# Second product of the next to last tile by seven block products, with the sums kept on the chip

## The chip, the cores and the metric

One NeuronCore of a Trainium2 chip runs the whole kernel. Time is device time in microseconds (us) of that core, as a median of several executions. TensorE (PE in the profile) multiplies matrices into PSUM; VectorE (DVE), ScalarE (ACT) and GpSimd (POOL) do what is elementwise; SyncE (SP) starts the transfers. Each engine works through its own queue in order and waits on semaphores for the others.

## The reference

Attention over 8 batches of 8 heads, 576 positions and 64 dimensions, with a causal window of 128 and a slope of the head on the distance, and behind it a feed-forward layer on all 4608 tokens:

```python
scores = scale * np.matmul(q, k.transpose(0, 1, 3, 2))
mask = (rel >= 0) & (rel < window)
scores = np.where(mask, scores + bias[None], -1000000000.0)
attn = np.exp(scores - np.max(scores, axis=-1, keepdims=True))
attn = attn / (np.sum(attn, axis=-1, keepdims=True) + 1e-09)
x = np.matmul(attn, v)                      # as 4608 tokens x 512
h = x @ w_in                                # 512 -> 2048
g = 0.5 * h * (1.0 + erf(h * inv_sqrt2))
out = (g @ w_out).astype(np.float32)        # 2048 -> 512
```

## The kernel before

The tokens are cut into nine tiles of 512 (`TT`), numbered `t` = 0 to 8. While tile t goes through the feed-forward layer, attention of the next batch is worked in between its steps, so that TensorE always has something to do; tiles 7 and 8 have no attention beside them any more. Every float32 operand of a product is split into a high and a low float16 half, and a product is made of three: high by high, low by high, high by low. The low half is `value * scale - high`, one instruction on VectorE (`low_part`, line 149 in the profile).

A tile's first product (`mlp_in`, line 600) makes 16 blocks `h` of 128 features by 512 tokens, 12 matmuls of 512 columns each, in four PSUM buffers that take turns (tag `mm`). ScalarE turns `h` into `g32` by Gelu and, in tile 7, into the high half too (lines 623, 627); VectorE makes the low half. The second product (`mlp_out`, line 661) makes 4 blocks of 128 tokens by 512 outputs, 48 matmuls of 512 columns each: 192 in a tile.

Tile 8 (`t == FAST`, `seven_all`) is different. Both of its products treat the operands as 2 by 2 blocks and take seven products of (sums of) blocks in place of eight. For that it needs, beside the blocks themselves:

- sums of the blocks of `w_in`, called T1 to T4, in four parts `d` = 0 to 3 (`sums_of_weights`);
- sums of the blocks of `w_out`, likewise (`sums_of_weights_out`), laid into buffers that attention no longer needs (`qbuf`, `kbuf`, `vbuf`, `e_main`);
- sums of the tile's own `x` (`sums_of_x`) and of its features (`Seven.sum`: S1 to S4).

A sum is built by adding high and low half to float32, four subtractions, a cast to the high half on ScalarE and a subtraction for the low half on VectorE. In the kernel before, all adds and subtractions are VectorE's. `sums_of_weights` writes its halves to a buffer in device memory (`stored`); from there T1 is copied over the block of `w_in` that it replaces, and T2, T3 and T4 are read back part by part (`stream`) while tile 8 runs. These calls are spread over tile 6's end and tile 7 by a list of steps (`PARTS_AT`, `SUMS_AT`). Inside `seven_all`, `p1` to `p7` are the seven products of a part of the first product (12 matmuls of 256 columns each); `u` and `v` are their PSUM buffers, and `p6` adds to `u` what `p1` has left there, so it has to wait until ScalarE has copied `u` out (line 826). The second product follows as seven products of 48 matmuls of 256 columns (line 901).

A scheduler that works from the code's order and its own estimates sets the order of each engine's queue; waits come from which tile is read and written.

Of the kernel before, what the change touches and what calls it, by code (L numbers as in the profile page):

```python
# [57 lines left out]
def attention_gelu_mlp(  # L58
# [520 lines left out]
    def tile_scales(t, ns):  # L579
# [7 lines left out]
        nc.vector.tensor_scalar(sg, sww[:, r], sx[t], 2.0 ** -(22 if t >= FAST else 21), op0=ALU.mult, op1=ALU.mult)  # L587
# [5 lines left out]
    def mlp_in(t, fc):  # L593
# [50 lines left out]
    o_ps = {}

    def mlp_out(t, tb, fc, first=0, last=NFC - 1):
# [18 lines left out]
        if fc == last:  # L665
# [4 lines left out]
            else:  # L670
# [9 lines left out]
    sums, streams, rooms, slots = [], [], [], []  # L680
    sums_out = [e.rearrange(p)[:, 0 : 8 * 512].rearrange("p (a k s f) -> p a k s f", a=2, k=2, s=4)
                for e, p in ((qbuf, "p a s -> p (a s)"), (kbuf, "p a s -> p (a s)"),
                             (vbuf, "p a h n d -> p (a h n d)"), (e_main, "p g a k -> p (g a k)"))]
# [21 lines left out]
    def sums_of_blocks(name, blocks, order, gate=None):  # L705

        r = pool.tile([P, NG, W], F32, tag="s", name=f"t{name}", bufs=2)
        r = r.rearrange("p g k -> p (g k)")[:, 0:1024].rearrange("p (s f) -> p s f", s=4)
# [11 lines left out]
        return r  # L720

    def halves_of_sums(dst, r):
        nc.scalar.copy(dst[0], r)
        nc.vector.tensor_tensor(out=dst[1], in0=r, in1=dst[0], op=ALU.subtract)
# [433 lines left out]
```

## Time and profile before

| | |
|---|---|
| median of 3 executions | 944.19 us (943.04 to 946.74) |
| the profiled execution | 947.36 us, of which the span from first to last instruction is 945.3 us |
| granted TensorE clock, mean | 0.984 of full speed |
| PE busy | 909.2 us, 96% of the span |
| DVE busy | 720.3 us, 76% |
| ACT busy | 546.5 us, 58% |
| POOL busy | 194.2 us, 21% |

A group `L661 PE MATMUL o<-wo,g 128*128 128x512 f16 x12` is line 661's matmuls that write tile `o` from `wo` and `g`, 128 partitions by 512 columns each, twelve in a row. In the timeline the first number is when the first of them began (us from the span's start), the second how long until the last ended; in brackets stands how long the engine had waited and for whom. Matmul ends are modelled, so the time from one start to the next is what is read of PE. [...]

### The profile page before, as it was taken

What the parts mean: (1) busy time and instruction counts of PE and PEld (TensorE: products, weight loads), DVE (VectorE), ACT (ScalarE), POOL (GpSimd) and SP (SyncE); (2) the same over time, 40 slices, a digit from 0 to 9 for tenths busy, and PEclk for the clock granted to TensorE, in tenths of its full rate; (3) what the DMA queues carried; (4) which work ended last, traced back from release to release, by engine and by line L of the source; (5) the groups of instructions that cost most, each with busy time, mean ns of one, the idle gap of its engine ahead of it and who ended that gap; (6) DMA issues with size and microseconds to landing.
All of it is one profiled execution on the core that took longest, in us unless ns stands there. A gap on an engine that the chain in (4) does not pass through costs nothing.

```text
span 945.3 us, 18563 instructions
## 1 busy us (share of the span) xinstructions
PE 909.2 (96%) x7356; PEld 475.2 (50%) x7356; DVE 720.3 (76%) x1445; ACT 546.5 (58%) x1146; POOL 194.2 (21%) x412
## 2 busy tenths in 40 slices
PE   6969999789999899999999999999999999999998
PEld 3544444444454345444454445444544444445887
DVE  6798989779876877678767877787656799991771
ACT  5977967776673565356435643564465526731760
POOL 1010000013101443135313531163125420000000
PEclk9889999999999999999999999999999999999999
DMA  9518532972446124614562346225302554300201
GB/s 317 212 45 259 209 105 67 203 191 61 90 126 165 36 57 83 187 43 79 96 162 68 62 101 174 69 51 99 86 13 51 91 116 146 90 34 23 79 24 45
DMA packets 185527, 99.63 MB, mean 105 GB/s; under 512 B 133344, under 2 KB 165216, under 8 KB 185312
## 3 DMA queue, kind: packets, MB, share of 16 engines
q1 hardware_dynamic: 185440, 98.45, 41.3%
q8 instruction: 57, 0.93, 0.4%
q14 instruction: 30, 0.25, 0.1%
HBM read 50.72 MB, written 13.63 MB: 68 GB/s over the span
## 4 chain that ended last, share of the span: by engine, by line
PE 68%; DVE 7%; ACT 5%; DMA 4%; issue 2%; SPq 1%; DVEq 0%; ACTq 0%
PE o L661 31%; PE h L600 22%; PE av L559 4%; PE sc L415 4%; DMA v<-vp 2%; PE u L789 2%; PE u_out L901 2%; PE v L789 2%; DMA et<-e_main 1%; ACT s L510 1%; DVE stv L217 1%; DVE vbuf L149 1%; DVE nmax L507 1%; ACT L623 1%; ACT vbuf L337 1%
## 5 line engine op out<-in xcount | busy, mean ns | idle before, releaser
L600 PE MATMUL h<-x,wi 128*128 128x512 f16 x1536 | 344.7, 382 | 6.5 <-ACT g L623 3.0
L661 PE MATMUL o<-wo,g 128*128 128x512 f16 x1080 | 244.7, 379 | 1.1 <-DVE wo L149 1.1
L600 PEld LDWEIGHTS <-wi 128*128 128x128 f16 x1536 | 148.2, 98 | 188.0 <-issue 14.2
L661 PEld LDWEIGHTS <-g 128*128 128x128 f16 x1440 | 136.0, 98 | 164.6 <-issue 3.0
L510 ACT ACTIVATE s<-s,nmax 128x192 f32<-128x192 f32 x252 | 111.2, 443 | 103.1 <-DVE nmax L507 99.5
L623 ACT ACTIVATE g<-h,gs 128x512 f32<-128x512 f32 x112 | 74.8, 685 | 81.0 <-PE h L600 57.4
L149 DVE SCALAR_TENSOR_TENSOR g<-g,sg,g 128x512 f16<-128x512 f32 (+1 forms) x128 | 101.9, 811 | 22.6 <-POOL g L625 19.4
L625 POOL TENSOR_SCALAR g<-g,sg 128x512 f16<-128x512 f32 x96 | 78.5, 823 | 193.4 <-ACT g L623 189.6
L149 DVE SCALAR_TENSOR_TENSOR e_main<-s,z,e_main 128x192 f16<-128x192 f32 x252 | 107.4, 469 | 14.1 <-POOL e_main L519 9.6
L519 POOL TENSOR_SCALAR e_main<-s,z 128x192 f16<-128x192 f32 x180 | 87.6, 506 | 85.4 <-ACT s L510 29.0
L415 PE MATMUL sc<-kbuf,qbuf 64*64 64x192 f16 (+1 forms) x1656 | 74.3, 261 | 9.8 <-DMA kbuf<-kp 4.5
L661 PE MATMUL o<-wo_first,g 128*128 128x512 f16 x360 | 83.2, 380 | 0.3 <-DMA wo_first<-wo 0.3
L437 DVE SCALAR_TENSOR_TENSOR s<-sc,cs,bias_h 128x384 f32<-128x384 f32 x112 | 63.7, 607 | 12.8 <-PE sc L415 12.6
L507 DVE TENSOR_REDUCE nmax<-s 128x5 f32<-128x960 f32 (+1 forms) x56 | 58.5, 1044 | 2.2 <-POOL s L442 0.2
L442 POOL MEMSET s<- 64x128 f32 (+1 forms) x112 | 19.2, 172 | 186.4 <-DVE s L437 185.7
L572 ACT ACTIVATE x<-av,cx 128x448 f16<-128x448 f32 (+6 forms) x52 | 23.6, 474 | 58.4 <-PE av L559 58.2
L415 PEld LDWEIGHTS <-qbuf 64*64 64x64 f16 x1512 | 35.9, 106 | 38.2 <-issue 35.5
L559 PE MATMUL av<-et,vbuf 128*64 128x128 f16 (+1 forms) x1680 | 45.2, 213 | 4.2 <-DMA et<-e_main 4.2
L559 PEld LDWEIGHTS <-vbuf 128*64 128x64 f16 x1680 | 42.1, 113 | 14.3 <-issue 9.0
L510 ACT ACTIVATION_READ_ACCUMULATOR s<-s,nmax 128x1 f32 x252 | 47.2, 187 | 0.0
L510 ACT ACT_TABLE_LOAD x29 | 37.2, 1283 | 7.8 <-DVE square L120 7.3
L623 ACT ACT_TABLE_LOAD x29 | 37.2, 1283 | 6.4 <-issue 2.9
(224 smaller groups left out, 1029.0 us busy)
## 6 DMA issues: line engine op xcount, KB each, us to landing
v<-vp SPq DMA_DIRECT2D x32, 320.0 KB, 5.1
out<-ob SPq DMA_DIRECT2D x35, 256.0 KB, 2.2
raw<-w_in SPq DMA_DIRECT2D x8, 1024.0 KB, 14.0
raw<-w_out SPq DMA_DIRECT2D x8, 1024.0 KB, 5.7
q<-qp SPq DMA_DIRECT2D x7, 1152.0 KB, 6.1
k<-kp SPq DMA_DIRECT2D x7, 1152.0 KB, 6.6
stored<-ts SPq DMA_DIRECT2D x32, 128.0 KB, 2.2
room<-stored SPq DMA_DIRECT2D x12, 256.0 KB, 2.7
```

The source lines that it names most:

```text
L149: nc.vector.scalar_tensor_tensor(out=dst, in0=src, scalar=scale, in1=high, op0=ALU.mult, op1=ALU.subtract)
L415: nc.tensor.matmul(ps[bank][o, n, 0:W], a, m, start=(i == 0), stop=(i == len(terms) - 1 and b > 0), skip_group_check=True,)
L437: nc.vector.scalar_tensor_tensor(out=s[:, bank[0] : bank[0] + k, :], in0=ps[bank][:, 0:k, 0:W], scalar=cs, in1=bias.broadcast_to([P, k, W] ...
L507: nc.vector.tensor_reduce(out=nmax[:, r], in_=s[:, r], axis=AX.X, op=ALU.max, negate=True)
L510: nc.scalar.activation(s[:, i, :], s[:, i, :], AF.Exp, bias=nmax[:, i : i + 1], accum_out=z[:, i : i + 1])
L519: nc.gpsimd.tensor_scalar(e[:, i, 0, c], s[:, i], z[:, i : i + 1], 1.0, op0=ALU.mult, op1=ALU.mult)
L559: nc.tensor.matmul(av[r, (j - blocks[0]) * QB : (j - blocks[0] + len(js)) * QB], v32s[b][:, hp, kb, r] if b < EXACT else vbuf[:, vi, hp, k ...
L600: nc.tensor.matmul(ph, wi[n][:, a, cc, k * P : (k + 1) * P], x[:, cc, b, :], start=(i == 0), stop=(i == 3 * NCC - 1),)
L623: nc.scalar.activation(g32, ph, AF.Gelu, scale=gsc[t, n])
L625: nc.gpsimd.tensor_scalar(g[:, r, 0], g32, gsg[t, n], 1.0, op0=ALU.mult, op1=ALU.mult)
L661: nc.tensor.matmul(o, both[:, a, c], wo[n][:, b, k, :], start=(fc == first and i == 0), stop=(fc == last and i == 2),)
L789: nc.tensor.matmul(ps[:, k * HT : (k + 1) * HT], w(a, i)[:, k * P : (k + 1) * P], m(b, i),  start=first and n == 0, stop=True, skip_group_ ...
```

## The change

The second product of tile 7 is also taken by seven products of blocks (`FAST_OUT = 7`, `seven_out`, which `seven_all` now shares): 336 matmuls of 256 columns where 192 of 512 stood. Tile 7's features go through a new `features`, which keeps them in float32 until a part is complete, then makes three of its four halves and four sums, S1 to S4. The sums of `w_out` are needed a tile earlier and are now all taken at the end of tile 6 and the start of tile 7. The sums of `w_in` may only be made once tile 7's first product has read `w_in`, so `sums_of_weights` runs during `seven_out(7)`, and `stored` and the transfers to and from it are gone: T1 goes straight into its place, T2 to T4 into free stretches of ten buffers (`room_for_halves`, `piece`). In `sums_of_blocks` one of the two adds goes to GpSimd, and all of `sums_of_x` but its last instruction does.

```diff
@@ tile_scales, features, out_scale
+FAST_OUT = 7
-        nc.vector.tensor_scalar(sg, sww[:, r], sx[t], 2.0 ** -(22 if t >= FAST else 21), op0=ALU.mult, op1=ALU.mult)
+        nc.vector.tensor_scalar(sg, sww[:, r], sx[t], 2.0 ** -(22 if t >= FAST else 23 if t >= FAST_OUT else 21), op0=ALU.mult, op1=ALU.mult)
+        if t >= FAST_OUT:
+            Sums(t, q).features(r, ph)
+            return
         g32 = pool.tile([P, TT], F32, tag="ob", name=f"g32_{t}_{fc}", bufs=3)
         nc.scalar.activation(g32, ph, AF.Gelu, scale=gsc[t, n])
-        if t + 1 < FAST:
-            nc.gpsimd.tensor_scalar(g[:, r, 0], g32, gsg[t, n], 1.0, op0=ALU.mult, op1=ALU.mult)
-        else:
-            nc.scalar.activation(g[:, r, 0], g32, AF.Copy, scale=gsg[t, n])
+        nc.gpsimd.tensor_scalar(g[:, r, 0], g32, gsg[t, n], 1.0, op0=ALU.mult, op1=ALU.mult)
...
-    stored = dram.tile([4, NWP // 2, P, 2, 2, 256], F16, name="stored")
...
+    def sums_of_blocks(first, second, quarter, dst, gate=None):
+        r = [turns[m].rearrange("p (j f) -> p j f", j=first[0].shape[1]) for m in range(2)]
         if gate is not None:
-            nc.vector.tensor_copy(r[:, 0, 0:1], gate)
-        for m, b in enumerate(blocks):
-            nc.vector.tensor_tensor(
-                out=r[:, 2 * m : 2 * m + 2], in0=b[0], in1=b[1], op=ALU.add
-            )
-        b11, b12, b21, b22 = (r[:, n] for n in order)
+            for m in range(2):
+                nc.vector.tensor_copy(r[m][:, 0, 0:1], gate)
+        for m, b in enumerate((first, second)):
+            engine = nc.gpsimd if m else nc.vector
+            engine.tensor_tensor(out=r[m], in0=b[0], in1=b[1], op=ALU.add)
+        b11, b12, b21, b22 = (quarter(r, n) for n in range(4))
         nc.vector.tensor_tensor(out=b11, in0=b12, in1=b11, op=ALU.subtract)
         nc.vector.tensor_tensor(out=b12, in0=b22, in1=b12, op=ALU.subtract)
         nc.vector.tensor_tensor(out=b22, in0=b22, in1=b11, op=ALU.subtract)
         nc.vector.tensor_tensor(out=b21, in0=b21, in1=b22, op=ALU.subtract)
...
+        for n, v in ((T1, b11), (T3, b12), (T2, b22), (T4, b21)):
+            hi, lo = dst(n)
+            nc.scalar.copy(hi, v)
+            nc.vector.tensor_tensor(out=lo, in0=v, in1=hi, op=ALU.subtract)
...
     def sums_of_x(t, i):
         x = x_tile(t)[:, 2 * i : 2 * i + 2]
-        r = pool.tile([P, 2, TT], F32, tag="v32", name=f"r{t}_{i}", bufs=1)
-        nc.vector.tensor_tensor(out=r, in0=x[:, :, 0], in1=x[:, :, 1], op=ALU.add)
+        r = next_of(pairs).rearrange("p (c n) -> p c n", c=2)
+        nc.gpsimd.tensor_tensor(out=r, in0=x[:, :, 0], in1=x[:, :, 1], op=ALU.add)
...
+        nc.gpsimd.tensor_tensor(out=a22, in0=a21, in1=a22, op=ALU.add)
+        nc.gpsimd.tensor_tensor(out=a21, in0=a11, in1=a21, op=ALU.subtract)
+        nc.gpsimd.tensor_tensor(out=a11, in0=a22, in1=a11, op=ALU.subtract)
+        nc.gpsimd.tensor_tensor(out=a12, in0=a12, in1=a11, op=ALU.subtract)
...
+        def features(self, r, ph):
+            t, d = self.t, self.d
+            hi, k = divmod(r, 2)
+            if k == 0:
+                held32[d, hi] = next_of(pairs).rearrange("p (k f) -> p k f", k=2)
+            v = held32[d, hi]
+            nc.scalar.activation(v[:, k], ph, AF.Gelu, scale=gsc[t, 2 * d])
+            if k == 0:
+                return
+            if hi == 0:
+                self.halved(0, 0, v[:, :, 0:HT])
+                return
+            a11, a21 = (held32[d, 0][:, :, n * HT : (n + 1) * HT] for n in range(2))
+            a12, a22 = (v[:, :, n * HT : (n + 1) * HT] for n in range(2))
+            self.halved(1, 0, a12)
+            self.halved(1, 1, a22)
+            self.three(a11, a21, a22)
+            self.sum(S4, a12, a12, a11, ALU.subtract)
...
+        if t >= FAST_OUT:
+            rest_of_v = room_for_features()
+            for fc in range(NFC):
+                mlp_in(t, fc)
+                if fc in PARTS_AT:
+                    sums_of_weights_out(parts.pop(0))
+                if fc in SUMS_AT:
+                    sums_of_x(t + 1, SUMS_AT.index(fc))
+            room_for_halves(rest_of_ld, rest_of_v)
+            for n, _ in enumerate(seven_out(t)):
+                if n + 1 < NWP // 2:
+                    sums_of_weights(n)
+                if n == 6:
+                    turns[:] = later[2:4]
+                    sums_of_weights(NWP // 2 - 1)
+            continue
```

Up to the last softmax of attention no engine's queue changes. Three places behind it matter. The first is VectorE's queue where tile 8 starts. Its first instruction there is the sum of tile 8's first block (before: line 831, after: line 886, `room_s<-v,room_s`). Before, this stood ahead of it, the last sums of `w_out` and the last output block of tile 7:

```order
L717 TENSOR_TENSOR to_1_10210<-to_1_10210 128x256
L718 TENSOR_TENSOR to_1_10210<-to_1_10210 128x256
L719 TENSOR_TENSOR to_1_10210<-to_1_10210 128x256
L724 TENSOR_TENSOR e_main<-to_1_10210,e_main 128x1024
L671 TENSOR_SCALAR ob_2_10207<-o_2_10149,so_9650 128x512
L831 TENSOR_TENSOR room_s_10293<-v_0_10316,room_s_10293 128x512
```

After, the sums of `w_in` of part 3 and three of tile 7's output blocks stand there (750 to 753 are the four subtractions, 757 the low halves, 973 the output):

```order
L750 TENSOR_TENSOR slots_9623<-slots_9623 128x2x256
L973 SCALAR_TENSOR_TENSOR ob_1_0_10310<-x_out,so_9619,room_s_9621 128x512
L973 SCALAR_TENSOR_TENSOR ob_1_1_10313<-y_out,so_9619,room_s_9621 128x512
L751 TENSOR_TENSOR slots_9623<-slots_9623 128x2x256
L757 TENSOR_TENSOR wi_770<-slots_9623,wi_770 128x2x256
L752 TENSOR_TENSOR slots_9623<-slots_9623 128x2x256
L757 TENSOR_TENSOR vbuf<-slots_9623,vbuf 128x512
L753 TENSOR_TENSOR slots_9623<-slots_9623 128x2x256
L757 TENSOR_TENSOR bias_h<-slots_9623,bias_h 128x512
L973 SCALAR_TENSOR_TENSOR ob_0_1_10379<-z_out,so_9619,room_s_9622 128x256 x2
L757 TENSOR_TENSOR e_main<-slots_9623,qbuf 128x512
L886 TENSOR_TENSOR room_s_9621<-v_0_10408,room_s_9621 128x512
```

The sums of `w_in` have moved from the first half of tile 7 to right ahead of tile 8, on the queue that tile 8's first sum has to pass.

The second place is ScalarE's queue at the same point of the program. Before, the copy of `u` that `p6` waits for (line 826) came behind the last output block of tile 7:

```order
L723 CAST e_main<-to_0_10174 128x1024
L669 ACTIVATE ob_1_10137<-o_1_10079,so_9650 128x512
L723 CAST e_main<-to_1_10210 128x1024
L669 ACTIVATE ob_3_10284<-o_3_10219,so_9650 128x512
L826 COPY room_s_10293<-u_0_10302 128x512
```

After, the same copy (now line 881) comes behind the casts of the sums of `w_in` (line 756):

```order
L756 CAST slots_9625<-room_s_9621 128x512
L969 ACTIVATE room_s_9621<-u_out,so_9619 128x512
L756 CAST wi_770<-slots_9623 128x2x256
L756 CAST vbuf<-slots_9623 128x512
L756 CAST bias_h<-slots_9623 128x512
L756 CAST qbuf<-slots_9623 128x512
L881 COPY room_s_9621<-u_0_10394 128x512
L871 ACTIVATE room_s_9621<-room_s_9621,gs_0_10384 128x512
```

The cast of `qbuf` needs VectorE's line 753 of part 3, so the copy of `u` now stands behind the whole of VectorE's queue up to there.

The third place is the end of GpSimd's queue. Before, its last work was attention's (line 519):

```order
L442 MEMSET s_3_9216 64x128 x2
L442 MEMSET s_3_9216 64x64 x2
L519 TENSOR_SCALAR e_main<-s_3_9216,z_3_9313 128x192 x9
L1154 UNCONDITIONAL_BRANCH
L1154 ISA
```

After, 18 instructions with two tensor operands follow it: four adds for `w_out`, two sums of `x` of five instructions each, four adds for `w_in`. This is the middle of them (748 is the add of `sums_of_blocks`, 779 to 784 are `sums_of_x`):

```order
L748 TENSOR_TENSOR room_9583<-wo_1563 128x1024
L748 TENSOR_TENSOR room_9583<-wo_1683 128x1024
L779 TENSOR_TENSOR room_s_9621<-x_8841 128x1024
L781 TENSOR_TENSOR room_s_9621<-room_s_9621 128x256
L782 TENSOR_TENSOR room_s_9621<-room_s_9621 128x256
L783 TENSOR_TENSOR room_s_9621<-room_s_9621 128x256
L784 TENSOR_TENSOR room_s_9621<-room_s_9621 128x256
L779 TENSOR_TENSOR room_9584<-x_8841 128x1024
```

GpSimd had nothing to do from there to the end of the program before.

## Rows read from the trace of the kernel before

**Rows 1.** The page, span and busy time of each engine.

```profile
span 945.3 us, 18563 instructions
PE 909.2 (96%) x7356; PEld 475.2 (50%) x7356; DVE 720.3 (76%) x1445; ACT 546.5 (58%) x1146; POOL 194.2 (21%) x412
```

**Rows 2.** Busy time by stretch: tile 7's two products, tile 8 in halves, end.

```profile
core 0: us, PE busy (x) PEld busy (x) DVE busy (x) ACT busy (x) POOL busy (x), PEclk, DMA share, GB/s
785.20:826.60 41.40, 41.40 (x194) 18.75 (x193) 41.11 (x73) 29.99 (x40) 0.00 (x0) 1.00 0.43 128
826.60:868.00 41.40, 41.40 (x193) 18.81 (x192) 24.70 (x43) 9.02 (x10) 0.00 (x0) 1.00 0.07 26
868.00:905.70 37.70, 37.70 (x347) 33.75 (x345) 25.16 (x39) 27.40 (x45) 0.00 (x0) 1.00 0.25 71
905.70:941.50 35.80, 35.80 (x329) 31.91 (x326) 14.75 (x22) 10.39 (x16) 0.00 (x0) 1.00 0.07 23
941.50:945.30 3.80, 0.06 (x1) 0.00 (x0) 0.88 (x2) 0.00 (x0) 0.00 (x0) 1.00 0.20 69
```

**Rows 3.** Timeline of PE from tile 7 on (start, length, group).

```profile
826.60 2.75 PE L661 MATMUL o<-wo_first,g 128*128 128x512 f16 x12
...
868.04 1.47 PE L789 MATMUL u<-x,wi 128*128 128x256 f16 x12
...
872.18 1.47 PE L789 MATMUL u<-room,room 128*128 128x256 f16 x12
...
922.73 0.82 PE L901 MATMUL u_out<-qbuf,slots 128*128 128x256 f16 x6
...
927.97 0.82 PE L901 MATMUL y_out<-vbuf,slots 128*128 128x256 f16 x6
```

**Rows 4.** Timeline of ACT, first copy of tile 8.

```profile
869.60 0.59 ACT L826 COPY room_s<-u 128x512 f32<-128x512 f32 x1 [0.68 <-PE u L789]
```

**Rows 5.** Timeline of DVE from attention's end to tile 8's features.

```profile
766.67 0.18 DVE L514 RECIPROCAL z<-z 128x4 f32<-128x4 f32 x1
...
793.81 2.35 DVE L724 TENSOR_TENSOR ts<-ti,ts 128x1024 f16<-128x1024 f32 x2
796.08 0.42 DVE L760 TENSOR_TENSOR r<-r 128x256 f32<-128x256 f32 x1
...
839.21 0.68 DVE L712 TENSOR_TENSOR to<-wo 128x512 f32<-128x512 f16 x1
839.81 0.74 DVE L671 TENSOR_SCALAR ob<-o,so 128x512 f32<-128x512 f32 x1
840.47 1.88 DVE L712 TENSOR_TENSOR to<-wo 128x512 f32<-128x512 f16 x3
...
912.59 0.69 DVE L819 TENSOR_TENSOR room_s<-room_s 128x512 f32<-128x512 f32 x1
913.31 0.69 DVE L819 TENSOR_TENSOR room_s<-s,room_s 128x512 f32<-128x512 f32 x1
...
915.18 1.40 DVE L149 SCALAR_TENSOR_TENSOR slots<-room_s,sg,slots 128x512 f16<-128x512 f32 x2
916.51 0.74 DVE L149 SCALAR_TENSOR_TENSOR g<-room_s,sg,g 128x512 f16<-128x512 f32 x1
```

**Rows 6.** Timeline of DVE in tile 5, low halves with POOL at work.

```profile
623.30 4.47 DVE L149 SCALAR_TENSOR_TENSOR g<-g,sg,g 128x512 f16<-128x512 f32 x4
```

**Rows 7.** Timeline of POOL, the same stretch, and one instruction ahead of it.

```profile
614.14 0.69 POOL L625 TENSOR_SCALAR g<-g,sg 128x512 f16<-128x512 f32 x1 [2.37 <-ACT g L623]
...
622.38 2.65 POOL L625 TENSOR_SCALAR g<-g,sg 128x512 f16<-128x512 f32 x3
625.35 0.79 POOL L625 TENSOR_SCALAR g<-g,sg 128x512 f16<-128x512 f32 x1 [0.31 <-ACT g L623]
626.45 0.78 POOL L625 TENSOR_SCALAR g<-g,sg 128x512 f16<-128x512 f32 x1 [0.31 <-ACT g L623]
```

More of the change, by code (lines that the diff above doesn't have):

```diff
@@ L672, in mlp_out @@
             nc.sync.dma_start(out[t * TT + tb * P : t * TT + (tb + 1) * P, :], ob)
-    stored = dram.tile([4, NWP // 2, P, 2, 2, 256], F16, name="stored")
     S2, S3, S4, S1 = range(4)
     T2, T3, T4, T1 = range(4)
[L680 to L683, printed above, removed]
+    sums, rooms, slots, turns, later, pairs, pieces = ([] for _ in range(7))
@@ L685, in room_for_sums @@
     def room_for_sums():
-        a, b = (pool.tile([P, NPAIR * S], F32, tag="ld", name=f"room{n}", bufs=2).bitcast(F16) for n in range(2))
+        a, b = (flat("ld", [P, NPAIR, S], F32, f"room{n}", 2) for n in range(2))
+        turns.extend(a[:, n * 1024 : (n + 1) * 1024] for n in range(2))
+        pairs.extend(b[:, n * 1024 : (n + 1) * 1024] for n in range(2))
+        a, b = a.bitcast(F16), b.bitcast(F16)
         x = a[:, 0 : 4 * NCC * HT].rearrange("p (i a s f) -> p i a s f", i=2, a=2, s=4)
@@ L700, in room_for_features @@
-        where.append(pool.tile([P, NPAIR, NKB, P], F32, tag="v32", name="slots2", bufs=1)
-                     .rearrange("p h n d -> p (h n d)").bitcast(F16))
+            pairs.append(s[:, 0:1024])
+            later.append(s[:, 0:1024])
+        where = [flat(f"et{n}", [P, NG * 4, P], F16, f"slots{n}", 1) for n in range(2)]
+        where.append(flat("v32", [P, NPAIR, NKB, P], F32, "slots2", 1).bitcast(F16))
+        later.extend(where[0].bitcast(F32)[:, n * 1024 : (n + 1) * 1024] for n in range(2))
@@ new lines, in room_for_halves @@
+    def room_for_halves(b, v):
+        x = pool.tile([P, NCC, 2, TT], F16, tag="x", name="room_x", bufs=2).rearrange("p c a f -> p (c a f)")
+        h = bias_h.rearrange("p h k -> p (h k)").bitcast(F16)
+        n = 512
+        halves = [(e[:, at : at + n], e[:, at + n : at + 2 * n]) for e, ats in (
+            (b, range(0, 8 * n, 2 * n)), (x, range(0, 8 * n, 2 * n)), (v, [8 * n]), (h, [0]), (spare[2], [8 * n]),
+        ) for at in ats]
+        halves.append((spare[0][:, 8 * n : 9 * n], spare[3][:, 8 * n : 9 * n]))
+        pieces.extend([a.rearrange("p (i f) -> p i f", i=2) for a in piece] for piece in halves)
+        turns[:] = later[0:2]
@@ L719, in sums_of_blocks @@
         nc.vector.tensor_tensor(out=b21, in0=b21, in1=b22, op=ALU.subtract)
[L720 to L724, printed above, removed]
-    def sums_of_weights(d, i, gate=None):
-        r = sums_of_blocks(f"i{d}_{i}", [
-            [wi[2 * d + m][:, a, 2 * i : 2 * i + 2] for a in range(2)] for m in range(2)
-        ], (0, 2, 1, 3), gate)
-        st = pool.tile([P, NG * 4, P], F16, tag=f"et{i}", name=f"ts{d}_{i}", bufs=1)
-        st = st.rearrange("p n f -> p (n f)")[:, 0:2048].rearrange("p (a s f) -> p a s f", a=2, s=4)
-        halves_of_sums([st[:, a] for a in range(2)], r)
-        for n, k in ((T1, 0), (T2, 3), (T3, 2), (T4, 1)):
-            nc.sync.dma_start(stored[n, d, :, :, i], st[:, :, k])
@@ L885, in seven_all, with seven_out @@
             q[d].p7()
-            if d < last:
-                stream(T3, d + 1)
+        for _ in seven_out(t, q[last]):
+            pass
+    def seven_out(t, rest=None):
+        last, every = NWP // 2 - 1, range(NWP // 2)
         ps = {}
@@ L1063, in attention_gelu_mlp @@
     SCORES_AT, WEIGH_AT = (2, 11, 16, 21), (12, 20, 25, 30)
-    PARTS_AT, SUMS_AT = (1, 3, 6, 9, 12, 15, 17, 19, 21, 23, 25, 27), (28, 29)
-    parts = [lambda d=d, i=i, gate=None: sums_of_weights(d, i, gate) for d in range(NWP // 2) for i in range(2)]
-    parts += [lambda d=d, k=k: sums_of_weights_out(d, k) for d in range(NWP // 2) for k in range(2)]
+    PARTS_AT, SUMS_AT = (2, 6), (10, 14)
+    parts = list(range(NWP // 2))
     for t in range(1, NTILE):
```

178 lines of the change are left out of this document (93 added, 85 removed).

## The prediction

> **What bounds the kernel now.** I read first the busy time of each engine [rows 1]: TensorE is busy for 909.2 of 945.3 us, VectorE for 720.3. That is a mean over stages, so I cut the part that the change touches into stretches [rows 2]. [...] VectorE is nearly full too in tile 7's first product, 41.11 of 41.40 us, and has room only in its second, 24.70 of 41.40. GpSimd does nothing at all from 785.20 on. So the gain is TensorE's in the second product of tile 7, and what can eat it is VectorE, to which the change gives more to do and less time to do it in.
>
> **What is removed.** The timeline of TensorE [rows 3] has tile 7's second product from 826.60 to 868.04, 41.44 us for 192 matmuls of 512 columns. Its seven products are 336 matmuls of 256 columns. Tile 8's second product has the same ones already: one product of 48 runs from 922.73 to 927.97, 5.24 us. Seven take 36.68 us, so TensorE's own time falls by 4.76 us. The transfers to and from the stored sums go as well; nothing on TensorE waits for one [rows 2], so I count them at nothing.
>
> **What VectorE has to do, and by when.** All sums and tile 7's features now stand in VectorE's queue between attention's last softmax and the start of tile 8. The end of this stretch is a chain: ScalarE's first copy of tile 8 (line 881, which `p6` waits for) stands behind the cast of part 3's last sum, and that cast waits for VectorE's line 753 of part 3.
>
> The time there is. It begins where VectorE has the last softmax's reciprocal, 766.67 and 0.18 long [rows 5]: 766.85, the gate of the first new sum. In the trace `p6` starts at 872.18, 4.14 us after tile 8's first matmul at 868.04 [rows 3]. Tile 8 would now start 4.76 us earlier, at 863.28, and want `p6` at 867.42. Ahead of that lie the copy, 0.59 us [rows 4], and a cast of as many elements, which I price the same. So line 753 has to end by 866.24, and VectorE has 99.4 us.
>
> The work. Prices are from one start to the next [rows 5]: 1.14 us for 1024 columns (two from 793.81 to 796.08), 0.60 for 512 with two tensors in (839.21 to 839.81), 0.66 for a low half (915.18 to 916.51 has two) or an output block (839.81 to 840.47). By the code, the queue up to there holds:
> - 10 of 1024 columns: eight adds of blocks and the two last instructions of `sums_of_x`: 11.4 us;
> - 78 of 512: 32 subtractions of weight sums, 30 of their low halves (two of part 3 come later), 16 sums of features: 46.8 us;
> - 28 low halves of tile 7's features, seven in each part: 18.5 us;
> - 16 left-overs: eight of attention, five output blocks, three of a few columns: about 6.9 us.
>
> Together 83.6 us. A subtraction that directly follows the one whose result it needs starts 0.72 us behind it (912.59 to 913.31), not 0.60. If all 48 subtractions did, this would be 5.8 us more; I reckon with a dozen and take 85.0 us, with 83.6 and 89.4 as ends. That fits into 99.4 with 14.4 to spare.
>
> **GpSimd beside it.** The change also wakes GpSimd in this stretch, and the trace shows that the two do not work beside each other for free. Alone, a low half follows another after 0.66 us, so four would take 2.72 us to the end of the last (three steps and its 0.74). With GpSimd at work four took 4.47 us [rows 6], 1.75 more; GpSimd ran four multiplications of 512 columns beside them, two of the three at 622.38 and those at 625.35 and 626.45, and these were slower too, 0.88 us for one of the three where one alone takes 0.69 [rows 7]. So each of GpSimd's instructions cost VectorE 0.44 us, or 0.86 ns per column, and they take turns. That instruction reads one tensor; the new ones read two, and the trace has none such. GpSimd gets eight adds of 1024 columns, and twice `sums_of_x` with one of 1024 and four of 256: 12,288 columns. If only the columns count, VectorE loses 10.6 us; if every tensor read does, 21.1 us. I take the second: if the two engines take turns at reading, the row prices one tensor read, and an add has two. Both ends stay for the range; a cost below the first would need an add that is cheaper than a multiplication, and nothing is gained from GpSimd beyond the instructions that I have left out of VectorE's list.
>
> One thing more: four adds for `w_in` have VectorE's first subtraction waiting for their result. GpSimd needs 0.69 us alone for what costs VectorE 0.44, so I add 0.25 for each, 1.0 us.
>
> By this VectorE needs 85.0 + 21.1 + 1.0 = 107.1 us of 99.4, and is late by 7.7 us. TensorE then waits for as long, mostly at `p6` of tile 8. A part of the lateness can show earlier, and is then not paid twice, since whatever TensorE waits in tile 7 moves the later date as well.
>
> [...]
>
> **Sum.** 7.7 - 4.76 = +2.9 us. The profiled execution took 947.36 us, the median of the three shown is 944.19; the change is the same length in both, so 950.3 for the one and 947.1 for the other. With VectorE's work at its ends it is 1.5 to 7.3 us more than before: 945.7 to 951.5.
>
> **Rivals.**
> - *VectorE is in time.* If an add costs VectorE only by its columns, it needs 85.0 + 10.6 + 1.0 = 96.6 us of 99.4, TensorE never waits, and all 4.76 us are gained: 939.4. For it: VectorE's list alone leaves 14.4 us, and parts of the sums could fall into gaps. Against it: the row of four low halves. The point where it turns is a cost to VectorE of 13.4 us for all of GpSimd's work, 1.1 us for an add of 1024.
> - *GpSimd holds VectorE for longer.* In the rows a multiplication costs VectorE 0.44 us and lasts 0.69 alone. If with two tensors the loop inside takes longer and the cost lies midway, at 0.565 us per 512 and tensor, 12,288 columns cost 27.1 us, VectorE is 13.7 late, and the kernel takes 8.9 us more: 953.1. With the full 0.69 it would be 33.1 us and 959, which I hold for unlikely, since the two overlapped in the row. [...]
> - *It bites before tile 8.* VectorE's queue runs through the low half of `x7`'s last pair, which the first block's last matmul needs, and through the sums of part 2, whose casts stand ahead of tile 7's first Gelu on ScalarE. Should VectorE be late there, TensorE waits in tile 7's first product. By itself that adds nothing, as said; only a wait of another kind, say a Gelu that finds no free buffer among the four of `pairs`, would come on top, 1 to 3 us: about 949.
>
> **How the numbers follow.** 0.5% is 4.7 us and about what a measurement of this kernel can tell from no change. My own case has 0.50; about 0.15 of it lies over 948.9, the rest within 0.5%. The longer hold has 0.20, all slower. VectorE in time has 0.25: at 939.4 it sits just at the lower bound, 939.5, so I give 0.10 to faster and 0.15 to within. The extra wait in tile 7 has 0.05, slower. That makes faster 0.10, within 0.50, slower 0.40. The range reaches from the full gain, 939.4, past the longer hold with some of VectorE's upper end, 955. The likeliest case alone is 945.7 to 951.5.
>
> **What the profile after would show.** Right: line 948's 336 matmuls take 36.7 us plus waits; TensorE, without a gap before, has one of some 8 us at tile 8's first `p6` (line 861) or spread over tile 7, and the chain of waits there leads over ScalarE to VectorE; GpSimd's adds of 1024 last about 2 us; low halves and subtractions beside them last clearly over 0.75 us. Wrong: adds of about 1.3 us and VectorE's instructions at their usual length, with no gap on TensorE; then the first rival holds. If VectorE is hardly slowed and still late, my list of its work was short; if GpSimd's add lasts over 2.5 us, the second rival holds.

## The result, and the profile after

The changed kernel takes 948.75 us (median of 16 executions, 946.6 to 953.03), the kernel before 944.54 us beside it (16 executions). The ratio is 1.0044, with a 95% interval of 1.003 to 1.0057: 4.2 us more. The forecast was 2.9 us more. The profiled execution took 946.64 us, 944.9 of them span. In it tile 7 begins at 779.29, not at 785.16; TensorE's work ahead of that is the same in both kernels and differed between two executions. So I compare by stage: from the start of tile 7 to the end it is 165.6 us here (944.9 - 779.29) and 160.1 before (945.3 - 785.16), 5.5 us more in this one execution (by the interval of the ratio it is 2.8 to 5.4). Tile 7's first product, before and after:

```profile
785.16 41.60 PE L600 MATMUL h<-x,wi 128*128 128x512 f16 x192
779.29 41.60 PE L600 MATMUL h<-x,wi 128*128 128x512 f16 x192
```

The page, against [rows 1]: VectorE has 22.0 us more, GpSimd 32.9, TensorE 6.2 less.

```profile
span 944.9 us, 18800 instructions
PE 903.0 (96%) x7500; PEld 488.1 (52%) x7500; DVE 742.3 (79%) x1427; ACT 556.4 (59%) x1175; POOL 227.1 (24%) x430
```

Busy time by stretch, against [rows 2]: tile 7's two products, then tile 8, and last a piece of the second product.

```profile
core 0: us, PE busy (x) PEld busy (x) DVE busy (x) ACT busy (x) POOL busy (x), PEclk, DMA share, GB/s
779.30:820.70 41.40, 41.40 (x193) 18.77 (x192) 39.24 (x51) 28.74 (x46) 11.86 (x7) 1.00 0.02 7
820.70:866.20 45.50, 39.93 (x338) 33.99 (x337) 43.42 (x50) 18.17 (x29) 16.72 (x9) 0.92 0.02 7
866.20:905.00 38.80, 37.50 (x344) 33.44 (x342) 31.20 (x50) 28.89 (x47) 0.00 (x0) 1.00 0.07 22
905.00:944.00 39.00, 36.21 (x332) 32.20 (x330) 15.98 (x25) 10.78 (x17) 0.00 (x0) 1.00 0.09 28
...
853.00:858.10 5.10, 5.09 (x25) 3.50 (x25) 4.98 (x4) 0.58 (x1) 2.61 (x1) 0.50 0.00 0
```

Most of the loss is in the second row; a wait of 1.46 us stands at the start of the third. The first product is as long as before. The second should take 36.68 us and takes 45.46 (820.73 to 866.19 in the next rows). In it TensorE has gaps, VectorE has almost none (43.42 of 45.50), GpSimd works for 16.72 us, and the granted clock is 0.92.

TensorE in its timeline, against [rows 3]:

```profile
820.73 0.82 PE L948 MATMUL u_out<-wo_first,g 128*128 128x256 f16 x6
...
853.01 1.44 PE L948 MATMUL u_out<-qbuf,slots 128*128 128x256 f16 x6 [4.72 <-ACT room_s L969]
854.24 1.48 PE L948 MATMUL u_out<-kbuf,slots 128*128 128x256 f16 x6
...
860.95 0.82 PE L948 MATMUL z_out<-wo_first,g 128*128 128x256 f16 x6
...
866.19 1.47 PE L861 MATMUL u<-x,wi 128*128 128x256 f16 x12
...
871.80 1.47 PE L861 MATMUL u<-room,room 128*128 128x256 f16 x12 [1.30 <-ACT room_s L881]
```

The third product into `u` comes 4.88 us late behind the one before it (from start to start; the bracket counts from the modelled end of the last matmul and is some 0.16 us shorter, as the profile has a matmul of 256 columns at 0.27 us and the next begins after 0.11) and then takes 7.94 us (853.01 to 860.95) where such a product takes 5.24 [rows 3]: its first groups of six start 1.23 to 1.28 us apart, not 0.65, and the last row above has a granted clock of 0.50 there, where tile 7's first product has 1.00. Tile 8's first `p6` waits another 1.46 us, and two gaps of 0.38 and 0.79 us stand further ahead. Waits of 7.51 us and 2.70 us of slower matmuls make 10.2 us; less the 4.76 us saved, that is the 5.5.

Who is late is seen one engine further on. ScalarE:

```profile
849.78 0.62 ACT L756 CAST wi<-room_s 128x512 f16<-128x512 f32 x1 [4.61 <-DVE room_s L750]
850.50 0.62 ACT L756 CAST room_x<-room_s 128x512 f16<-128x512 f32 x1
851.75 0.62 ACT L756 CAST room<-room_s 128x512 f16<-128x512 f32 x1 [0.63 <-DVE room_s L752]
852.28 0.68 ACT L969 ACTIVATE room_s<-u_out,so 128x512 f32<-128x512 f32 x1
...
870.65 0.62 ACT L756 CAST qbuf<-slots 128x512 f16<-128x512 f32 x1 [0.58 <-DVE slots L753]
871.17 0.58 ACT L881 COPY room_s<-u 128x512 f32<-128x512 f32 x1
```

Both copies that TensorE waits for, that of tile 7's second product into `u` (`c2` in the code, line 969) and that of tile 8's first block (line 881), stand in ScalarE's queue behind casts of sums (line 756), and these wait for VectorE. VectorE and GpSimd at the same places, and ahead of them the reciprocal with which VectorE's list begins:

```profile
760.17 0.18 DVE L514 RECIPROCAL z<-z 128x4 f32<-128x4 f32 x1
...
811.94 2.62 DVE L149 SCALAR_TENSOR_TENSOR g<-room_s,sg,g 128x512 f16<-128x512 f32 x1
...
845.92 3.03 DVE L748 TENSOR_TENSOR room_s<-wi 128x1024 f32<-128x1024 f16 x1
...
857.28 1.21 DVE L748 TENSOR_TENSOR slots<-wi 128x1024 f32<-128x1024 f16 x1
...
869.93 0.68 DVE L753 TENSOR_TENSOR slots<-slots 128x512 f32<-128x512 f32 x1
```

```profile
811.44 2.57 POOL L779 TENSOR_TENSOR room_s<-x 128x1024 f32<-128x1024 f16 x1 [19.33 <-DVE slots L149]
814.09 1.05 POOL L781 TENSOR_TENSOR room_s<-room_s 128x256 f32<-128x256 f32 x1
...
845.26 2.60 POOL L748 TENSOR_TENSOR room_s<-wi 128x1024 f32<-128x1024 f16 x1 [5.74 <-DVE room L757]
```

A low half that takes 0.74 us alone [rows 5] takes 2.62 beside GpSimd's add, and VectorE's own add of 1024 columns takes 3.03 where it takes 1.21 without (at 857.28): some 1.8 us more in either case. That is the mechanism of the forecast; the runs below try it.

### The profile page after: what moved, and what is told of

It is laid out like the page before. It is cut to its first block, busy times and chain, and to the rows that moved or that the text cites. A ratio compares the mean times of both kernels' runs of the same rounds, so it can differ in the third digit from the quotient of the medians.

```text
span 944.9 us, 18800 instructions
## 1 busy us (share of the span) xinstructions
PE 903.0 (96%) x7500; PEld 488.1 (52%) x7500; DVE 742.3 (79%) x1427; ACT 556.4 (59%) x1175; POOL 227.1 (24%) x430
## 4 chain that ended last, share of the span: by engine, by line
PE 54%; DVE 17%; ACT 6%; DMA 5%; issue 3%; POOL 1%; SPq 1%; DVEq 0%; POOLq 0%; ACTq 0%
PE o L661 24%; PE h L600 15%; PE av L559 3%; PE sc L415 3%; DMA v<-vp 3%; DMA et<-e_main 2%; PE u L861 2%; PE u_out L948 2%; PE v L861 2%; DVE stv L217 1%; DVE g L149 1%; DVE vbuf L149 1%; ACT s L510 1%; ACT vbuf L337 1%; DVE s L437 1%
## 5 line engine op out<-in xcount | busy, mean ns | idle before, releaser
L661 PE MATMUL o<-wo,g 128*128 128x512 f16 x936 | 214.5, 382 | 0.7 <-DVE wo L149 0.5
L661 PEld LDWEIGHTS <-g 128*128 128x128 f16 x1248 | 117.6, 98 | 142.1 <-issue 3.9
L510 ACT ACTIVATE s<-s,nmax 128x192 f32<-128x192 f32 x252 | 111.2, 442 | 102.3 <-DVE nmax L507 99.6
L626 ACT ACTIVATE g<-h,gs 128x512 f32<-128x512 f32 x96 | 63.8, 686 | 74.6 <-PE h L600 51.8
L149 DVE SCALAR_TENSOR_TENSOR g<-g,sg,g 128x512 f16<-128x512 f32 (+1 forms) x112 | 90.4, 824 | 21.5 <-POOL g L627 19.4
L661 PE MATMUL o<-wo_first,g 128*128 128x512 f16 x312 | 71.8, 379 | 0.0
L948 PEld LDWEIGHTS <-g 128*128 128x128 f16 x384 | 37.4, 98 | 5.9 <-DVE g L149 1.4
```

What stands on the lines that cost most here:

```text
L149: nc.vector.scalar_tensor_tensor(out=dst, in0=src, scalar=scale, in1=high, op0=ALU.mult, op1=ALU.subtract)
L510: nc.scalar.activation(s[:, i, :], s[:, i, :], AF.Exp, bias=nmax[:, i : i + 1], accum_out=z[:, i : i + 1])
L661: nc.tensor.matmul(o, both[:, a, c], wo[n][:, b, k, :], start=(fc == first and i == 0), stop=(fc == last and i == 2),)
L948: nc.tensor.matmul(ps[name][:, tb], f(d, a)[:, k, tb * P : (tb + 1) * P], w(d, b, k), start=first, stop=True, skip_group_check=True,)
```

## The experiments

Theory A is that of the prediction: GpSimd's instructions with two tensors hold VectorE up, and VectorE's list ends late. Rival B: VectorE's own list is too long, and GpSimd beside it costs nothing. Rival C: the order of ScalarE's queue (copies behind casts) makes the wait by itself. Rival D: the lower clock is a cost of its own. Each ratio is to the kernel before on the same chip. Two numbers of each profile tell most: how long after the first matmul of tile 7's second product the first `p6` of tile 8 starts, and how long VectorE takes from the end of attention's last reciprocal to the end of the last subtraction for part 3 of `w_in` (in the changed kernel 760.35 to 870.61).

| kernel | ratio (95% interval) | to `p6`, us | in time would be | VectorE's list, us |
|---|---|---|---|---|
| changed kernel | 1.0044 (1.003 to 1.0057) | 51.07 | 40.82 | 110.3 |
| 1: all sums on VectorE | 0.9972 (0.9955 to 0.9988) | 41.92 | 41.92 | 101.6 |
| 2: one tensor read | 0.9976 (0.9959 to 0.9993) | 43.14 | 40.82 | 102.3 |
| 3: own bank | 1.0096 (1.0072 to 1.012) | 52.32 | 41.27 | 111.5 |
| 5: filled gap | 1.0074 (1.0045 to 1.0103) | 51.48 | 40.82 | 110.7 |
| 6: all on VectorE, rooms exchanged | 0.9954 (0.9936 to 0.9972) | 40.83 | 40.82 | 101.6 |
| 7: adds of blocks on VectorE | 0.999 (0.9979 to 1.0002) | 44.42 | 41.92 | 104.7 |
| 8: rooms exchanged alone | 1.0051 (1.0036 to 1.0067) | 50.99 | 40.82 | 110.2 |

In time is 36.68 us plus the 38 matmuls that stand ahead of `p6` (4.14 us); in runs 1 and 7 the order of tile 8 has 48 there (5.24 us), in run 3 it has 42 (4.59 us), and the 40 that fill the gap in run 5 are not counted. Run 4 has more instructions at its end, so its time isn't compared.

In the changed kernel and in runs 2 to 5 and 8, `p6` starts 1.19 us after the end of VectorE's list, a cast and a copy later, to within 0.01 us. In runs 1, 6 and 7 the scheduler, which orders every queue anew, has put the copy for `p6` ahead of the cast of `qbuf`, the last one; there the end of the list doesn't set `p6`.

**1. All sums on VectorE.**

```diff
-            engine = nc.gpsimd if m else nc.vector
-            engine.tensor_tensor(out=r[m], in0=b[0], in1=b[1], op=ALU.add)
+            nc.vector.tensor_tensor(out=r[m], in0=b[0], in1=b[1], op=ALU.add)
...
-        nc.gpsimd.tensor_tensor(out=r, in0=x[:, :, 0], in1=x[:, :, 1], op=ALU.add)
+        nc.vector.tensor_tensor(out=r, in0=x[:, :, 0], in1=x[:, :, 1], op=ALU.add)
```

(and so the other four of `sums_of_x`).

> Every sum that the change gave to GpSimd (eight adds of blocks, both sums of x) is on VectorE, nothing else differs. In the changed kernel TensorE waited 7.5 us from tile 7's second product to tile 8's first p6 and ran 2.7 us longer at the lower clock. Theory A, GpSimd's two-tensor instructions hold VectorE up: by the groups of VectorE's instructions they cost it about 18 us and 1 us of waiting; the same work on VectorE costs 10 instructions of 1024 columns at 1.22 us and 8 of 256 at about 0.35, 15 us. So the lateness falls by about 4 us, TensorE waits 2 to 5 us, the clock loss shrinks, and the time is 940 to 944, a ratio to before of 0.995 to 1.000. Rival B, VectorE's own list is too long and GpSimd works beside it for nothing: 15 us more work on VectorE make the wait 22 us, ratio 1.018. Rival C, the order of ScalarE's queue makes the wait: c2's wait stays at 4 to 5 us and the ratio at 1.004.

Measured: 941.03 us against 943.7, ratio 0.9972. VectorE has 18 instructions more and is done 8.7 us sooner. `p6` comes in time, and TensorE does not wait in tile 7 at all:

```profile
865.98 1.47 PE L860 MATMUL u<-room,room 128*128 128x256 f16 x12
```

B falls: more work on VectorE did not make it later. C is not decided here, for ScalarE's order changed too: the first copy below (`c2`) now stands ahead of the casts of part 1 and waits for TensorE alone, and the copy for `p6` stands ahead of the cast of `qbuf`.

```profile
845.22 0.69 ACT L968 ACTIVATE room_s<-u_out,so 128x512 f32<-128x512 f32 x1 [3.33 <-PE u_out L947]
845.80 0.61 ACT L755 CAST wi<-room_s 128x512 f16<-128x512 f32 x1
...
864.87 0.58 ACT L880 COPY room_s<-u 128x512 f32<-128x512 f32 x1 [0.93 <-PE u L860]
865.35 0.62 ACT L755 CAST qbuf<-slots 128x512 f16<-128x512 f32 x1
```

A's direction holds, its amount was set too low: 4 us were expected, 8.7 came. What TensorE still loses is in tile 8, where the queues now have another order:

```profile
874.67 1.47 PE L860 MATMUL u<-x,room 128*128 128x256 f16 x12 [0.67 <-ACT s L899]
...
888.88 0.39 PE L947 MATMUL z_out<-wo_first,g 128*128 128x256 f16 x2 [0.95 <-ACT g L797]
```

**2. One tensor read.**

```diff
-            engine = nc.gpsimd if m else nc.vector
-            engine.tensor_tensor(out=r[m], in0=b[0], in1=b[1], op=ALU.add)
+            if m:
+                nc.gpsimd.tensor_scalar(r[m], b[0], 1.0, 0.0, op0=ALU.mult, op1=ALU.add)
+                continue
+            nc.vector.tensor_tensor(out=r[m], in0=b[0], in1=b[1], op=ALU.add)
```

> GpSimd's eight adds of blocks become a multiplication by 1.0 of the high half alone: same columns, same output, one tensor read instead of two. It leaves the low half of these weights out of the sums, so the output is a little less exact. Sums of x stay as they are. Theory A with the price by tensors read (0.86 ns per column and tensor): each of the eight costs VectorE 0.88 us instead of about 1.8, the lateness falls by 7 us, TensorE waits under 1.5 us, ratio 0.995 to 0.998. Theory A with a hold for as long as GpSimd's instruction lasts, whatever it reads: each costs 1.3 us, TensorE waits 3 to 4 us, ratio 0.998 to 1.000. Rivals B and C: nothing changes for VectorE or ScalarE's order, ratio 1.003 to 1.006.

Measured: 942.08 us, ratio 0.9976. The same number of GpSimd's instructions over the same columns, with one tensor in place of two, moves `p6` forward by 7.9 us, 1.0 us for each of the eight. A single wait of 2.3 us is left, at `p6`, between the two forms of A:

```profile
866.80 1.47 PE L863 MATMUL u<-room,room 128*128 128x256 f16 x12 [2.15 <-ACT room_s L883]
```

B is refuted once more, since VectorE has the same instructions. C is refuted here: `c2` still stands behind three casts of part 1 and the copy for `p6` behind that of `qbuf`, and with VectorE sooner the wait at the first is gone and both waits together are 2.3 us, not 6.3.

**3. Own bank.**

```diff
-        add("u", sum_of_features(S3), sum_of_weights(T3), every)
-        plus(c2, "y", c2)
-        c3 = copy("u")
+        if rest:
+            add("u", sum_of_features(S3), sum_of_weights(T3), every)
+            plus(c2, "y", c2)
+            c3 = copy("u")
+        else:
+            add("u3", sum_of_features(S3), sum_of_weights(T3), every)
+            c3 = rooms[copies.pop(0)].rearrange("p (b f) -> p b f", b=2)
+            plus(c3, "u3", c2)
+            plus(c2, "y", c2)
```

(`rest` is set in tile 8 alone, so only tile 7 is changed.)

> Tile 7's third u product goes to a PSUM bank of its own and is added on VectorE, so that it no longer waits for ScalarE's copy c2 behind the casts; VectorE has one instruction more (0.74 us) in place of ScalarE's third copy. Theory A, VectorE is late by about 7.5 us at the end of its list, and where TensorE waits for it is only a matter of which product comes to it first: the 4.9 us gap at the third u product goes, and tile 8's first p6 waits 6 to 8 us instead of 1.5. The sum of waits stays at 7 to 8.5 us, the time within 0.2% of the changed kernel, apart from 2.7 us if the clock holds. Rival C, the order of ScalarE's queue makes the wait: the gap goes and nothing takes its place, waits of 2 to 3 us in all, and the time falls by 5 to 7.5 us, ratio to before 0.996 to 0.999.

Measured: 951.28 us, ratio 1.0096. The gap in tile 7 is gone, and the whole lateness stands at `p6`, where the prediction had put it:

```profile
872.22 2.72 PE L861 MATMUL u<-room,room 128*128 128x256 f16 x12 [9.67 <-ACT room_s L881]
```

C's forecast, that nothing takes the gap's place, is refuted, and so is my own bound of 0.2%: the kernel became 0.5% slower than the changed one. `p6` comes 1.25 us later (VectorE's list is 1.2 us longer), and from there to the end it takes 75.4 us (947.6 - 872.22) where the changed kernel takes 73.1: the twelve matmuls of the row take 2.72 us, not 1.47, at a granted clock of 0.50 (872.20 to 877.50), now where nothing hides it. The gaps sum to 11.0 us, not 7 to 8.5.

**4. Prices at the end of the program.** After the last output of the changed kernel stand stretches like these, in words of the code: into which buffer GpSimd writes, what VectorE does and how often, what GpSimd does and how often. Each begins and ends with a copy of VectorE, so that GpSimd's work lies inside it:

```diff
+    stretch(lb[:, 0:1024], two, 12, add_two, 4)
+    stretch(lb[:, 1024:2048], two, 12, mul_one, 4)
+    stretch(sa[:, 0:1024], one, 12, add_two, 4)
+    stretch(sb[:, 0:1024], two, 12, add_two_256, 8)
```

> The changed kernel, with a stretch appended after its last output, which prices VectorE's instructions of 512 columns alone and beside GpSimd's, each in a group of its own: two-tensor VectorE beside 4 two-tensor adds of 1024; beside 4 one-tensor multiplications of 1024; one-tensor VectorE beside 4 two-tensor adds; two-tensor VectorE beside 8 adds of 256; then GpSimd alone. The total time says nothing. Theory A by tensors read: VectorE loses 1.8 us for an add of 1024 and 0.9 for a multiplication of 1024. Theory A by the length of the instruction: VectorE loses nearly the whole 2.1 to 2.6 us of an add, about 1.3 of a multiplication, and 1.0 of an add of 256. Rival B: VectorE's 12 instructions take 12 times 0.60 to 0.68 us wherever they stand.

VectorE's timeline (line 1204 has two tensors, 1207 one; the first groups of each are alone):

```profile
947.00 5.78 DVE L1204 TENSOR_TENSOR price<-price,price 128x512 f32<-128x512 f32 x8 [0.87 <-DMA out<-ob]
...
952.99 15.86 DVE L1204 TENSOR_TENSOR price<-price,price 128x512 f32<-128x512 f32 x12
968.95 0.15 DVE L1215 COPY price<-price_b 128x1 f32<-128x1 f32 x1
969.14 3.66 DVE L1207 TENSOR_SCALAR price<-price 128x512 f32<-128x512 f32 x8
...
973.02 11.54 DVE L1204 TENSOR_TENSOR price<-price,price 128x512 f32<-128x512 f32 x12
...
985.03 12.67 DVE L1207 TENSOR_SCALAR price<-price 128x512 f32<-128x512 f32 x12
...
998.18 11.91 DVE L1204 TENSOR_TENSOR price<-price,price 128x512 f32<-128x512 f32 x12
```

GpSimd's, beside VectorE and, in the last three, alone:

```profile
953.10 10.12 POOL L1218 TENSOR_TENSOR price_b<-price_x 128x1024 f32<-128x1024 f16 x4 [91.72 <-DVE price_b L1210]
973.08 5.86 POOL L1221 TENSOR_SCALAR price_b<-price_x 128x1024 f32<-128x1024 f16 x4 [9.86 <-DVE price_b L1210]
985.15 9.04 POOL L1218 TENSOR_TENSOR price_s<-price_x 128x1024 f32<-128x1024 f16 x4 [6.21 <-DVE price_s L1210]
998.23 9.13 POOL L1224 TENSOR_TENSOR price_s<-price,price 128x256 f32<-128x256 f32 x8 [4.04 <-DVE price_s L1210]
1010.61 4.31 POOL L1218 TENSOR_TENSOR price_b<-price_x 128x1024 f32<-128x1024 f16 x2 [3.25 <-DVE price_b L1210]
1015.38 2.17 POOL L1221 TENSOR_SCALAR price_b<-price_x 128x1024 f32<-128x1024 f16 x2 [0.46 <-DVE price_b L1210]
1018.01 1.52 POOL L1224 TENSOR_TENSOR price_s<-price,price 128x256 f32<-128x256 f32 x2 [0.46 <-DVE price_s L1210]
```

Alone, VectorE starts an instruction of 512 columns every 0.725 us (two tensors, each writing over the result of the last) or 0.46 (one). Twelve take 8.70 or 5.53 us. Beside four adds of 1024 columns the twelve take 15.96 us (952.99 to the copy at 968.95), so an add costs VectorE 1.82 us. A multiplication with one tensor costs it 0.74 (11.64 us to its copy at 984.66), an add of 256 columns 0.41 (12.01 us to 1010.19, eight of them). The forecast had priced the add of 1024 at 1.76, by two tensors of 0.86 ns per column, and that of 256 at 0.44; the multiplication, by one tensor, it would have priced at 0.88. B is refuted directly.

**5. The gap filled.** 40 matmuls whose result nobody uses.

```diff
+FILL = 40
...
+        if not rest:
+            fill = psum.tile([P, 2, DM // 2], F32, tag="att", name="fill", bufs=4)
+            for n in range(FILL):
+                nc.tensor.matmul(
+                    fill[:, 0], g_of[t, 0][:, 0, 0, 0:P], wo[0][:, 0, 0, 0 : DM // 2],
+                    start=True, stop=True, skip_group_check=True,
+                )
         add("u", sum_of_features(S3), sum_of_weights(T3), every)
```

> The changed kernel with 40 more matmuls of 256 columns into an unused PSUM bank, placed on TensorE between tile 7's fourth block product y and its third u product, so that TensorE works (4.4 us) where it waited 4.9 us for ScalarE's copy c2. Their result is used by nobody. In the changed kernel's profile the third u product then ran 2.7 us longer, with a granted clock of 0.91 over the stretch. Theory A, VectorE's list alone sets when tile 8's first p6 may start (VectorE has no gap in the changed kernel from 837 to 873): the third u product takes 5.2 us again, the wait at p6 grows from 1.5 to about 4 us, p6 starts 51.0 to 51.5 us after tile 7's second product as before, and the ratio to before stays at 1.003 to 1.006 (up to 1.008 if the clock falls in the longer wait at p6). Rival D, the clock is a cost of its own beside the waits: the wait at p6 stays at 1.5 us, p6 starts 2.7 us earlier, ratio 1.000 to 1.003.

Measured: 951.08 us, ratio 1.0074. The third `u` product takes its 5.2 us again, and `p6` comes no sooner:

```profile
853.00 0.82 PE L949 MATMUL u_out<-qbuf,slots 128*128 128x256 f16 x6 [0.36 <-ACT room_s L970]
...
858.23 0.82 PE L949 MATMUL z_out<-wo_first,g 128*128 128x256 f16 x6
...
872.17 2.72 PE L862 MATMUL u<-room,room 128*128 128x256 f16 x12 [4.38 <-ACT room_s L882]
```

D is refuted: the 2.70 us of slower matmuls lay under VectorE's lateness. TensorE, now at a granted clock of 1.00 (825 to 865), only waits longer at `p6` (4.38 us in the bracket), and there the clock falls instead (0.50 from 872.2 to 875.0), where it costs something (74.5 us from `p6` to the end, 1.4 more).

**6. All sums on VectorE, rooms exchanged.** `rooms` are stretches of the two buffers `room_s`, three of each, into which ScalarE copies the products of tile 8; sums of `w_in` are built in the first two of the three. Run 1, and:

```diff
-            self.s1 = rooms[3 * (self.d % 2)]
+            self.s1 = rooms[3 * (self.d % 2) + 2]
...
-            s4 = rooms[3 * (self.d % 2) + 2]
+            s4 = rooms[3 * (self.d % 2)]
```

> Every sum on VectorE as in the first experiment, and tile 8's first and fourth products use each other's room (s1 the third, s4 the first of the three), so that ScalarE's copy of part 0's first product need not wait until the sums of w_in have left the first room; with it the order of tile 8 begins with part 0 again. In the first experiment TensorE ran tile 7 without a wait and lost 1.8 us in three waits of tile 8 and 0.6 us beside them. Theory A: VectorE's list is as long as there and just in time; the waits of tile 8 shrink to under 1 us, and the time is 939 to 941, ratio 0.995 to 0.997, at best the 4.76 us that the products save. Rival: VectorE is so near its limit that p6 of part 0, which now comes first, waits for it 1 to 2 us; ratio 0.997 to 0.999, no better than the first experiment.

Measured: 939.82 us against 944.21, ratio 0.9954, 4.3 us less than before. From tile 7's start TensorE has no gap left:

```profile
779.40:820.90 41.50, 41.50 (x194) 18.83 (x193) 41.01 (x62) 30.23 (x47) 0.00 (x0) 1.00 0.02 7
820.90:857.50 36.60, 36.60 (x337) 32.82 (x336) 36.19 (x52) 15.98 (x26) 0.00 (x0) 1.00 0.07 23
857.50:894.50 37.00, 37.00 (x341) 33.16 (x340) 29.89 (x48) 27.03 (x45) 0.00 (x0) 1.00 0.03 8
```

So the saving of the seven products is real, and this version beats both kernels. Two things bring it about: VectorE's list is 8.7 us shorter, and the copy for `p6` stands ahead of the last cast. With the list alone `p6` would by estimate still be 1.6 us late (101.6 + 1.19 - 60.38 us from the reciprocal to the second product, less 40.82). Against run 1 the times alone don't decide (the intervals overlap); the trace shows its three waits gone.

**7. Only the adds of blocks on VectorE.** The first half of run 1's edit.

> Only the eight adds of blocks are on VectorE; both sums of x stay on GpSimd (two adds of 1024 columns, eight of 256). In the changed kernel tile 8's first p6 starts 51.1 us after tile 7's second product; in time would be 40.8, so VectorE is 10.3 us late there. Theory A with the prices of the fourth run: each of the eight adds saves VectorE 1.82 - 1.22 = 0.60 us and four of them a wait of about 0.25 as well, 5.8 us; the sums of x go on holding it 2 x 1.82 + 8 x 0.41 = 6.9 us in tile 7. So VectorE is still 3 to 5 us late, TensorE waits that long, p6 starts 44 to 46 us after tile 7's second product, and the ratio is 0.997 to 1.001, between the changed kernel and the first experiment. Rival: only GpSimd's adds in the second product matter (the adds of w_in), since the sums of x stand in a part where VectorE has room; then p6 is in time and the ratio is that of the first experiment or better, 0.995 to 0.9975.

Measured: 942.44 us against 943.39, ratio 0.999. VectorE's list is 5.6 us shorter than in the changed kernel, by the prices 5.8; `p6` comes at 44.42 us after a wait of 2.5 us. The wait is under the 3 to 5 us expected, as in this order ten more matmuls stand ahead of `p6` and its copy no longer stands behind the last cast. The sums of `x` count: without them VectorE is 3.1 us sooner (run 1), though one of the two stands in tile 7's first product.

**8. Rooms exchanged alone.** The diff of run 6, on the changed kernel.

> The changed kernel with its sums on GpSimd as they were, and only the rooms of tile 8's first and fourth products exchanged as in the sixth run. Theory A, VectorE's end of its list sets p6: nothing changes there, p6 starts 50.5 to 51.5 us after tile 7's second product, ratio 1.003 to 1.006. Rival: in the sixth run it was the rooms that won the time, as ScalarE's copy for p6 no longer waits for the sums in its room; then p6 starts at least 1.5 us earlier and the ratio falls to 1.000 to 1.003.

Measured: 947.3 us against 943.39, ratio 1.0051; `p6` at 50.99 us, with the same two waits of 4.9 and 1.5 us. While VectorE is late the rooms change nothing. ScalarE's order did not change by them either; what the sums on GpSimd would cost with the copies ahead of the casts, as in run 6, no run shows.

## Why the prediction was right, and where it was off

- **The matmuls saved.** 4.76 us, confirmed: the second product takes 36.68 us wherever TensorE isn't kept waiting (820.85 to 857.53 in run 6), and run 6 gains 4.3 us over the whole kernel.
- **VectorE's list.** Forecast 85.0 us. In run 6 VectorE works from the reciprocal on with 0.13 us of gaps of over 0.1 us and needs 101.6 us; the 18 instructions that GpSimd had take some 15.0 of them by their rows there (eight adds at 1.18 from start to start, two sums of `x` at 2.98 and 2.57). That leaves 86.6: the forecast was 1.6 us too low.
- **GpSimd's price.** Forecast 21.1 us held up and 1.0 waited for, 22.1. Measured 23.7: the 110.3 of the changed kernel less 86.6. Of this some 18 us are seen as longer instructions (busy time over count times median, by shape) and 4.2 as gaps of over 0.1 us; some 1.5 I have not placed. What I had too low was the waiting around the instructions, 1.0 us. The price of an add came out right (1.82 against 1.76), its reason did not: by tensors read a multiplication would cost half of an add, and it costs 0.74 of 1.82. That the two engines take turns was my reading of [rows 6] and [rows 7]; what they share no run shows. Run 4 has the times: VectorE's twelve and GpSimd's four adds, 8.70 and 8.62 us alone, take 15.96 beside each other. That the add of 1024 columns, the one that carries most of the sum, lies so near its price is in part luck.
- **The time there is.** Forecast 99.4 us. It was 100.0, since the last reciprocal came 0.63 us earlier beside TensorE's work: 60.38 us ahead of tile 7's second product (820.73 - 760.35), before 59.75 (826.60 - 766.85). This date holds for ScalarE's order in the changed kernel; in run 6 the list ends 1.6 us after it, and TensorE does not wait.
- **The sum.** VectorE is late by 110.3 - 100.0 = 10.3 us, which is TensorE's 51.07 - 40.82; forecast 7.7. The mechanism was right, the lateness mis-sized by 2.6 us: 1.6 from GpSimd's work, 1.6 from the list, less 0.6 of time gained.
- **Where it shows.** I wrote "mostly at `p6` of tile 8". It showed mostly at the third `u` product of tile 7. I had followed ScalarE's queue only at the start of tile 8; the copy `c2` stands behind casts just the same, and TensorE comes to it earlier. That costs nothing more, as the prediction said of any place ahead of `p6`; run 3 shows the place moved, and the time not won.
- **The clock.** Not foreseen. In the changed kernel it stands under VectorE's lateness (run 5); after a wait at `p6` it costs 1.4 to 2.3 us (runs 3 and 5).
- **The rivals.** VectorE in time at the cost of columns alone: refuted, an add costs 1.82 us, over its turning point of 1.1. The longer hold: refuted, it wanted 2.26 us for an add of 1024 (0.565 us per 512 and tensor). The sign that I had named for it, an add of over 2.5 us, did show: five of GpSimd's ten take 2.57 to 3.03 us in the changed kernel. The sign was badly chosen, for GpSimd's add is itself longer beside VectorE (2.53 us from start to start in run 4) than alone (2.15), while VectorE loses 1.82. An extra wait in tile 7's first product: none, TensorE is busy there for all 41.40 us.

In the changed kernel the loss falls on single instructions: VectorE's add at 845.92 takes 3.03 us beside GpSimd's at 845.26, and the subtraction behind it, at 849.05, takes 0.69 again.

## What to carry to other kernels

Work given to GpSimd relieves VectorE only if it takes more time on VectorE than it costs it there: an add of two tensors of 1024 columns is 1.22 us on VectorE, and on GpSimd still takes 1.82 us from it (run 4). Before work is moved to an idle engine, look in the trace for a place where the two already run side by side and compare the pitch of the same instruction with and without. And ask for the engine whose list ends last: taking away the wait that the profile names (run 3), or filling it (run 5), moves the wait on as long as that list is as long and the work that others wait for stands behind its end. So read the queues of every variant again: moving work between two engines (run 1) also changed the order on a third.

## What the hardware showed beyond this

- In run 4, what GpSimd's instruction costs VectorE is its own length when alone, less about a third of a microsecond, in all three kinds: 2.15 and 1.82 us, 1.09 and 0.74, 0.76 and 0.41. The multiplications of 512 columns in [rows 6] and [rows 7] have a quarter less, 0.69 and 0.44.
- VectorE's instructions with a single tensor (line 1207) are held as long as those with two: 1.81 us for an add (12.78 us for twelve of run 4, 5.53 alone).
- GpSimd pays too: its add of 1024 columns takes 2.53 us beside VectorE, 2.15 alone; one of 256 columns 1.14 and 0.76.
- After pauses of 4.72, 9.67 and 4.38 us, as the brackets have them (changed kernel, runs 3 and 5), TensorE came back at a granted clock of 0.50 (853.0 to 858.1, 872.2 to 877.5 and 872.2 to 875.0); after the 1.30 us at `p6` in the changed kernel and the 2.15 us of run 2 it was 1.00 (871.8 to 875.0, 866.8 to 870.0). In the changed kernel the third `u` product lost 2.70 us by it (7.94 against 5.24).
